# A last product with 640 channels to a partition: column groups of 32 and one store per half group

## The chip, the cores and the metric

The kernel runs on one core of one Trainium2 chip. The metric is the device time of one execution in microseconds; the median of three runs of the kernel before is 315.18 us (315.0 to 315.5). A core has five engines that run side by side and wait for each other through semaphores: PE (TensorE, matrix products; its weight loads are shown as PEld), DVE (VectorE), ACT (ScalarE), POOL (GpSimd) and SP (SyncE, which here only issues transfers). Sixteen DMA engines move data between DRAM and the on-chip memory SBUF, whose 128 rows are called partitions. PE writes its products to PSUM, a second on-chip memory of 128 partitions, and ACT or DVE read them from there.

## The reference

Two branches of the same input x (2048 tokens x 640 channels) are mixed by a gate per token:

```
x = A_x
g = sigmoid((x * gate_w).sum(-1, keepdims=True))
a = A_ref(x, wqkv, wo)        # 32 heads, each token attends to 8 tokens at a distance of 0, 2, ... 14
b = B_ref(x, ...)             # y = irfft(rfft(x, 4096) * rfft(K, 4096))[:2048] + x * Dskip, per channel
return g * a + (1 - g) * b
```

K is a filter per channel, K[d, l] = Re sum_n C[d,n] exp(dt A[d,n] l) dt B[d,n] over 192 states. The result is 2048 x 640 in bf16, 2.62 MB.

## The kernel before, in words

The kernel has two parts. The first ("main") loads x and the weights, does the attention, multiplies it by the gate, g * a, and stores that in a DRAM buffer gaS (2048 x 640, lines 487 to 506); it also stores 1 - g in omS, builds the filter K and does the first stage of the transforms. The second ("tail", the function fft_conv) finishes the long convolution and mixes. Only its end concerns the change.

The transform of 4096 points is split. A token number is t = 64 a + t2, with a from 0 to 31 and t2 from 0 to 63. In the tail, blocks fb = 0 to 7 do the second stage of the forward transforms (L1095) and the product of the two spectra on DVE (L1123, L1126). Then 20 groups of PE products (L1156) do the first inverse stage; ACT and DVE bring each from PSUM to the tile C, which lies in the buffer bufA (L511, L513). C holds, on 128 partitions, four blocks of 160 channels with 32 frequencies each: partition 32 g + f.

The last product goes from the 32 frequencies to the 32 values of a, for each t2. Its weights psi come from DRAM in four loads of 0.5 MB; a 64 x 64 weight block holds two copies of a 32 x 32 matrix on its diagonal, one for each channel block on the 64 rows, with zeros elsewhere. Before the change a product of 64 rows, 64 output columns and 160 moving columns (L1186) makes two channel blocks for one t2 at a time, in different halves of the output's 64 partitions. PE takes four of them side by side: r = 0, 1 picks the half of the rows, j = 0, 1 the half of the output columns. So an output partition is (j, channel half, a), and holds for each of its 32 tokens (t2 = 32 j + u) a row of 320 channels. The order of the channel blocks, BLOCK = (0, 2, 1, 3) at line 33, is what makes the two blocks on one partition neighbours. It is applied where x is loaded (L1026) and in the constants of the first stage (L981).

Twelve steps of two or three u each follow (TILES, L968). Each step has one PSUM tile yp of two banks out of four such tiles. "A" steps: ACT multiplies by 1 - g of the token (tile om32, one value per partition and u, L1192) into tt, and DVE adds the attention part gaF (L1195) in one go. "D" steps: DVE does both from PSUM at once (L1200). The steps write eight result tiles ot0 to ot7 of 2, 2, 6, 6, 6, 6, 2 and 2 rows, and each result tile leaves in four transfers of 32 partitions (L1213): SP issues two, POOL the other two (ACT for the last tile). A block of memory in these transfers is a row of 320 channels, 640 B.

gaF is gaS brought back into the layout of the output partitions, in eight loads of 320 KB on SP's queue (L1114), paced by the blocks fb = 3 to 6 of the forward transform. They follow the psi loads (L1111) and stand ahead of the output stores. The values 1 - g come the same way in four tiny loads on POOL's queue (L1029).

What sets the order: every step is a task of a plan (class Plan), and a string of numbers per plan (ORDER, line 54) gives the order in which tasks are recorded; the instructions of one engine run in that order. The durations and dues in the plan have no effect at run time. Waits follow from the data: an instruction waits for the writers of what it reads and the readers of what it overwrites.

Of the kernel before, what the change touches and what calls it, by code (L numbers as in the profile page):

```python
# [20 lines left out]
S = 2048  # L21
D = 640
# [7 lines left out]
SC = 512  # L30
NWARM = 22
NSC = S // SC
BLOCK = (0, 2, 1, 3)
WRDY, XRDY = (11.8, 16.0, 19.4), (8.6, 13.7, 26.7, 29.2)


# [4 lines left out]
def _attn_consts():  # L41
# [923 lines left out]


NF = 4096
TILES = ("A2", "D2", "A3 D3", "A3 A3", "D3 A3", "A3 A3", "A2", "D2")  # L968


def _fft_consts():
    w = lambda e: np.exp(-2j * np.pi * e / NF)
    t1 = np.arange(32); t2 = np.arange(64); f1 = np.arange(32); f2 = np.arange(64)
    F1 = w(64 * np.outer(t1, f1 + 0.5))
    f1c = np.zeros((32, 32, 2), np.float32)
    f1c[:, :, 0] = F1.real; f1c[:, :, 1] = F1.imag
    f1b = np.zeros((4, 32, 4, 64), np.float32)
    for g in range(4):
        f1b[g, :, g, :] = f1c.reshape(32, 64)
    f1c = f1b.reshape(128, 256)  # L980
    f1k = f1b.reshape(4, 8, 4, 256)[list(BLOCK)].transpose(1, 0, 2, 3).reshape(128, 256)  # L981
    Phi = w(t2[None, :, None] * (f1[:, None, None] + 0.5 + 64 * f2[None, None, :]))
    phis = np.zeros((64, 2, 32, 3, 2, 64), np.float32)
    for c2 in range(2):
        phis[:, c2, :, 0, c2, :] = Phi.real.transpose(1, 0, 2)
        phis[:, c2, :, 1, c2, :] = Phi.imag.transpose(1, 0, 2)
        phis[:, c2, :, 2, c2, :] = -Phi.imag.transpose(1, 0, 2)
    phis = phis.reshape(128, 32, 3, 128)
# [12 lines left out]


def fft_prefetch(ctx, tc, x, omS, keep):
    nc = tc.nc
    f1c_np, f1k_np, phi_np, gab_np, _ = _fft_consts()
    pre = ctx.enter_context(tc.tile_pool(name="ff_pre", bufs=1))
# [1 line left out]
    P["F1c"] = pre.tile([128, 256], BF16, name="F1c")  # L1008
    P["F1k"] = keep.tile([128, 256], BF16, name="F1k")
    P["GAB"] = pre.tile([128, 2, 128], BF16, name="GAB")  # L1010
    P["omF"] = pre.tile([128, 32], BF16, name="omF")
    P["xn"] = pre.tile([128, 8, D], BF16, name="xn", tag="uga")
    P["bufA"] = pre.tile([128, 20480], BF16, name="bufA")
    phi_d = nc.inline_tensor(phi_np, name="c_phi").ap()
# [7 lines left out]
    def rows(n):  # L1022
        g, h = n // 2, n % 2
        if n == 0:
            P["Usb"] = pre.tile([128, 64, 160], BF16, name="Usb", tag="uga")
        nc.gpsimd.dma_start(P["Usb"][32 * g:32 * g + 32, 32 * h:32 * h + 32], x.rearrange("(a b) d -> a b d", b=64)[:, 32 * h:32 * h + 32, 160 * BLOCK[g]:160 * BLOCK[g] + 160])  # L1026

    def gates(g):
        nc.gpsimd.dma_start(P["omF"][32 * g:32 * g + 32], omS.rearrange("(a c s) -> c a s", c=2, s=32)[g // 2])  # L1029

    def consts(_):
        nc.gpsimd.dma_start(P["F1c"][:], nc.inline_tensor(f1c_np, name="c_f1").ap())
# [13 lines left out]
def fft_conv(ctx, tc, P, big, now, pa, b, gaS, out2d):  # L1046
# [7 lines left out]
    sb = ctx.enter_context(tc.tile_pool(name="ff_sb", bufs=1))  # L1054
    Y = sb.tile([128, 2, 80, 128], BF16, name="Y")
    yv = Y[:].rearrange("p r x (g f) -> p r (x g) f", g=4)
    om32 = sb.tile([128, 32], F32, name="om32")
    psi = sb.tile([128, 64, 2, 64], BF16, name="psi")
    nc.vector.tensor_copy(om32[:], omF[:])
    gaF = P["pool"].tile([128, 32, 320], BF16, name="gaF", tag="uga")  # L1060
    gr = gaS.rearrange("(a c s) (g e) -> c g a s e", c=2, s=32, g=2)
    orr = out2d.rearrange("(a c s) (g e) -> c g a s e", c=2, s=32, g=2)
    phis, q = P["phis"], {}
    a, c = ExitStack(), ExitStack()
    wk = a.enter_context(tc.tile_pool(name="ff_wk", bufs=2, side="right"))
# [10 lines left out]
    for fb in range(8):  # L1076
# [32 lines left out]
        def paced(_, fb=fb):  # L1109
            if fb < 4:  # L1110
                nc.sync.dma_start(psi[:, 16 * fb:16 * fb + 16], psi_d[:, 16 * fb:16 * fb + 16])  # L1111
            for k in ((), (), (), (0,), (1, 2), (3, 4), (5, 6, 7), ())[fb]:
                j, h = k // 2, 16 * (k % 2)
                nc.sync.dma_start(gaF[32 * j:32 * j + 32, h:h + 16], gr[j // 2, j % 2][:, h:h + 16])  # L1114
# [30 lines left out]
    for cb in range(20):  # L1145
# [18 lines left out]
    prev, u0 = None, 0  # L1164
    tiles = [(o, c, k[0], int(k[1])) for o, c in enumerate(TILES) for k in c.split()]
    ends_, out_ = {}, {}
    for n, (o, chunk, en, w) in enumerate(tiles):
        us = range(u0, u0 + w)
        cw = sum(int(k[1]) for k in chunk.split())
        out_.setdefault(o, u0)  # L1170
        k0 = u0 - out_[o]
        u0 += w

        def fin(_, n=n, us=us, w=w, o=o, cw=cw):
            if n == 0:
                a.close(); big.close(); c.close()
                q["yps"] = ctx.enter_context(tc.tile_pool(name="ff_ps4", bufs=4, space=PSUM))
                q["wk"] = ctx.enter_context(tc.tile_pool(name="ff_wk2", bufs=6, side="right"))
            if ("ot", o) not in q:
                q["ot", o] = q["wk"].tile([128, cw, 320], BF16, name=f"ot{o}", bufs=1)  # L1180
            yp = q["yp", n] = q["yps"].tile([128, 2, 512], F32, name="yp")
            for k, u in enumerate(us):
                for ro in range(2):
                    for j in range(2):
                        for r in range(2):
                            nc.tensor.matmul(yp[64 * j:64 * j + 64, r, 160 * k:160 * k + 160], psi[64 * r:64 * r + 64, 32 * j + u, ro, :], C[64 * r:64 * r + 64, 64 * ro + 32 * j + u, :],  # L1186
                                             start=(ro == 0), stop=(ro == 1), skip_group_check=True, tile_position=(64 * r, 64 * j))

        def scale(_, n=n, us=us):
            t = q["tt", n] = q["wk"].tile([128, 3, 320], BF16, name="tt")  # L1190
            for k, u in enumerate(us):
                nc.scalar.activation(t[:, k].rearrange("p (r d) -> p r d", r=2), q["yp", n][:, :, 160 * k:160 * k + 160], ACT.Identity, scale=om32[:, u:u + 1])  # L1192

        def mix(_, n=n, us=us, w=w, o=o, k0=k0):
            nc.vector.tensor_tensor(q["ot", o][:, k0:k0 + w], q["tt", n][:, 0:w], gaF[:, us[0]:us[0] + w], ALU.add)  # L1195

        def both(_, n=n, us=us, o=o, k0=k0):
            for k, u in enumerate(us):
                r2 = lambda t: t.rearrange("p (r d) -> p r d", r=2)
                nc.vector.scalar_tensor_tensor(r2(q["ot", o][:, k0 + k]), q["yp", n][:, :, 160 * k:160 * k + 160], om32[:, u:u + 1], r2(gaF[:, u]), ALU.mult, ALU.add)  # L1200
        m = prev = pl.add(f"yp{n}", "P", 0.17 * w, fin, deps=cps, after=[prev] + (ends + paces + list(muls.values()) if n == 0 else []), acq=["yp"])
        if en == "D":
            os = pl.add(f"st{n}", "D", 0.46 * w, both, deps=[m], rel=[("yp", m)])
        else:
            v = pl.add(f"tt{n}", "A", 0.41 * w, scale, deps=[m], rel=[("yp", m)])
            os = pl.add(f"mx{n}", "D", 0.06 + 0.167 * w, mix, deps=[v])
        ends_.setdefault(o, []).append(os)
    for o, v0 in out_.items():
        q["w", o] = w = sum(int(k[1]) for k in TILES[o].split())

        def store(e, o=o, v0=v0, w=w):
            for j in ((0, 1) if e == "S" else (2, 3)):
                {"S": nc.sync, "G": nc.gpsimd, "A": nc.scalar}[e].dma_start(orr[j // 2, j % 2][:, v0:v0 + w], q["ot", o][32 * j:32 * j + 32, 0:w])  # L1213
# [219 lines left out]
```

## Time and profile before

| | |
|---|---|
| median of three runs | 315.18 us (315.0 to 315.5) |
| the profiled execution | 316.68 us, its span 314.9 us |
| PE, DVE, ACT busy | 286.3, 285.9, 285.2 us (91% each) |
| mean granted PE clock | 0.978 |
| HBM read, written | 29.60 MB, 14.01 MB |
| last product: first and last matrix product starts | 297.0 and 304.6 us |
| ACT scaling tiles (L1192), first and last start | 297.6 and 306.2 us |
| output stores issued by SP (L1213), first and last | 299.3 and 310.0 us |

The span runs from the first to the last instruction of one profiled execution. A row of the timeline gives the start, the length, the engine, the line, the operation, out<-in, and how many instructions are merged; "SPq", "POOLq" and "ACTq" are instructions of the queue itself, such as the issue of a transfer. Packets are the pieces in which DMA engines move data; a block of memory that is contiguous on both sides is one piece on the hardware queues (q1 is SP's, q10 is ACT's), while q0, POOL's, may put several together.

### The profile page before, as it was taken

Reading aid. Unit: us, or ns where it says so; the run is one execution under the profiler, and the core shown is the slowest. Engines: PE = TensorE matmul, PEld = TensorE weight load, DVE = VectorE, ACT = ScalarE, POOL = GpSimd, SP = SyncE. Lnnn points to the kernel's source line nnn. Section 1 sums busy time; section 2 is a strip of 40 time slices with the busy share of each in tenths; the row PEclk is TensorE's granted clock in tenths of the full one; section 3 lists DMA queues with packets and bytes.
Section 4 is the critical chain, followed back from the end, with each engine's and each line's share of the span. In section 5 each row is a group of like instructions: output and inputs, shape, how many; then the busy total and the mean of one; then the engine's idle time right before and its main releaser. Section 6 shows DMA issues by size and latency. Waiting matters only on the chain. (4 is left out here: it accounts for less than half of the span.)

```text
span 314.9 us, 12073 instructions
## 1 busy us (share of the span) xinstructions
PE 286.3 (91%) x5268; PEld 169.8 (54%) x5268; DVE 285.9 (91%) x381; ACT 285.2 (91%) x431; POOL 56.9 (18%) x84
## 2 busy tenths in 40 slices
PE   8799999999999999999999989789999999979740
PEld 3455543444554554555555555447668676659730
DVE  4988999999999989999999999999888899998881
ACT  2789869999999999999999999999989799997890
POOL 8722440302000001111302022020120000000072
PEclk9799999999999999999999999999999999997995
DMA  7995679286111304537795694742493366591076
GB/s 260 363 237 140 183 200 168 81 176 149 24 36 21 106 8 122 108 89 214 192 264 126 127 212 94 153 103 79 169 334 115 131 214 167 113 167 20 4 174 161
DMA packets 47182, 45.70 MB, mean 145 GB/s; under 512 B 27034, under 2 KB 40650, under 8 KB 47130
## 3 DMA queue, kind: packets, MB, share of 16 engines
q1 hardware_dynamic: 40776, 26.68, 32.7%
q0 software_dynamic: 5392, 17.53, 21.7%
q8 instruction: 41, 0.67, 0.9%
q10 hardware_dynamic: 962, 0.73, 0.8%
q14 instruction: 11, 0.09, 0.1%
HBM read 29.60 MB, written 14.01 MB: 138 GB/s over the span
## 5 line engine op out<-in xcount | busy, mean ns | idle before, releaser
L319 PE MATMUL tb<-bufA 128*128 128x512 bf16 x300 | 76.4, 390 | 1.6 <-DMA bufA<-in_A_wqkv_dram 1.2
L842 ACT ACTIVATE big<-ar 128x740 bf16<-128x740 int16 (+1 forms) x72 | 57.6, 876 | 0.2
L827 PE MATMUL ar<-Rarg,L 64*128 64x212 bf16 (+4 forms) x600 | 47.8, 251 | 5.0 <-ACT big L842 2.2
L844 ACT ACTIVATE big<-ar 128x848 bf16<-128x848 f32 x60 | 49.8, 903 | 0.5 <-PE ar L827 0.2
L319 PEld LDWEIGHTS <-bufA 128*128 128x128 bf16 x300 | 31.8, 121 | 30.3 <-issue 9.9
L453 DVE TENSOR_TENSOR pv<-vc,asb 128x2048 bf16<-128x2048 bf16 x40 | 47.7, 1217 | 0.2 <-PE tb L460 0.2
L827 PEld LDWEIGHTS <-L 64*128 64x128 bf16 x600 | 20.7, 94 | 33.7 <-issue 30.8
L864 DVE TENSOR_TENSOR pt<-big 128x1024 bf16<-128x1024 bf16 x48 | 32.2, 702 | 1.5 <-PE kps L882 0.8
L882 PEld LDWEIGHTS <-pt 128*32 128x32 bf16 (+1 forms) x2560 | 23.1, 92 | 11.6 <-issue 9.4
L882 PE MATMUL kps<-qq,pt 128*32 128x21 bf16 (+1 forms) x2560 | 28.1, 174 | 0.6 <-ACT E L511 0.3
L484 PE MATMUL tb<-wo_sb,oT 128*128 128x320 bf16 x160 | 27.7, 301 | 0.9 <-ACT ga L493 0.7
L384 DVE TENSOR_TENSOR prod<-qA,kA 128x2048 bf16<-128x2048 bf16 x20 | 23.8, 1219 | 0.4 <-PE lg L390 0.3
L511 ACT ACTIVATE sp_u<-fp 128x640 bf16<-128x640 f32 x30 | 22.4, 876 | 1.7 <-PE fp L1095 1.7
L384 DVE TENSOR_TENSOR prod<-prj 128x2048 bf16<-128x2048 bf16 x20 | 23.8, 1218 | 0.0
L460 PE MATMUL tb<-pv,ind 128*64 128x512 bf16 (+1 forms) x192 | 22.3, 350 | 0.3 <-DVE pv L453 0.3
L511 ACT ACTIVATE sp_k<-fp 128x640 bf16<-128x640 f32 x30 | 22.2, 883 | 0.4 <-PE fp L1095 0.4
L866 DVE TENSOR_TENSOR qq<-big 128x1344 bf16<-128x1344 bf16 x24 | 21.2, 884 | 0.0
L1213 POOL DMA_DIRECT2D out_dram<-ot x14 | 7.8, 560 | 71.3 <-PE yp L1186 68.8
L1095 PEld LDWEIGHTS <-PHI 128*128 128x128 bf16 x160 | 15.6, 98 | 7.8 <-issue 1.8
L377 POOL DMA_DIRECT2D vc<-vS x16 | 11.5, 726 | 44.5 <-DVE pv L453 39.6
L484 PEld LDWEIGHTS <-oT 128*128 128x128 bf16 x160 | 13.5, 97 | 8.1 <-issue 3.6
L493 ACT ACTIVATE ga<-tb,g_sb 128x320 bf16<-128x320 f32 x28 | 15.2, 570 | 0.0
(171 smaller groups left out, 525.6 us busy)
## 6 DMA issues: line engine op xcount, KB each, us to landing
vc<-vS POOLq DMA_DIRECT2D x16, 327.5 KB, 5.4
gaS<-ga SPq DMA_DIRECT2D x8, 320.0 KB
Usb<-in_A_x_dram POOLq DMA_DIRECT2D x8, 320.0 KB, 5.0
gaF<-gaS SPq DMA_DIRECT2D x8, 320.0 KB
bufA<-in_A_wqkv_dram SPq DMA_DIRECT2D x3, 800.0 KB
L<-Sprm SPq DMA_DIRECT2D x76, 30.0 KB
asb<-aS SPq DMA_DIRECT2D x16, 128.0 KB
psi<-c_psi SPq DMA_DIRECT2D x4, 512.0 KB
```

The lines of the kernel that those rows point to most:

```text
L319: nc.tensor.matmul(ppf, self.wq[:, which, kt, e::5], self.xT[:, c0 // 1024, kt, c0 % 1024:c0 % 1024 + SC], start=(kt == 0), stop=(kt == NK ...
L384: nc.vector.tensor_tensor(b[e][:], q[:, e, o:o + C].unsqueeze(1).to_broadcast([128, W, C]), win(k[:, e, :], o, W, DIL, C), ALU.mult)
L453: nc.vector.tensor_tensor(o, vw, b["asb"][:].unsqueeze(2).to_broadcast(sh), ALU.mult)
L460: nc.tensor.matmul(b["op", e][64 * a:64 * a + 64, 0:n, :], ind[:, 32:96], b["pv", e][:, w, a, 0:n, :], start=(w == 0), stop=(w == 3), skip ...
L484: nc.tensor.matmul(apf[:, :320], b["oT"][:, e, i * 128:(i + 1) * 128], wo_sb[:, e, hf * 320:(hf + 1) * 320], start=(e == 0), stop=(e == 4))
L511: nc.scalar.activation(o, i, ACT.Identity)
L827: nc.tensor.matmul(ar[:, g2, a0:a0 + ncol], L[rows, sb, gv, l0:l0 + 128], R[rows, c0:c0 + ncol], start=True, stop=True, tile_position=(64 ...
L842: nc.scalar.activation(d_[:, :, s0 * QW:s1 * QW], ar[:].bitcast(I16)[:, :, 0:2 * (s1 - s0) * QW:2], ACT.Sin, scale=SCL)
L844: nc.scalar.activation(dst[:, gp::2].rearrange("p g s n -> p g (s n)"), ar[:, :, 0:2 * EW], ACT.Exp)
L864: nc.vector.tensor_tensor(pt[:, :, k, :], gg[:, :, ::-1] if k else gg, e1, ALU.mult)
L866: nc.vector.tensor_tensor(qq[:], trg[:, :, KI:].rearrange("p a (v m) -> p a v m", v=2), exq[:, :, KI:].unsqueeze(2).to_broadcast([128, 32, ...
L882: nc.tensor.matmul(kps[32 * g:32 * g + 32, h, NM * ql:NM * ql + NM], pt[rows, k, v, :], qq[rows, k, v, :], start=(g not in started), stop= ...
```

## The change

The last product is laid out by whole rows. There are now 16 steps, one for each u from 0 to 15, with t2 = 16 j + u and j = 0 to 3. A product has 64 rows, 32 output columns and 160 moving columns; four column groups j and two row halves r stand side by side, and an outer loop g picks the channel block on the 64 rows by taking 32 of the 64 weight columns. So an output partition is (j, a) and holds 16 tokens of 640 channels; a PSUM tile yp holds one u: 320 channels in each of its two banks. There are 512 products with their weight loads in place of 256. BLOCK is gone, since the channel blocks are now in natural order.

ACT scales 640 channels in one instruction (11 in place of 22), DVE does five direct tiles of 640 in place of ten of 320, and seven adds of 640 or 1280 in place of eight of 640 or 960. The share of ACT and DVE in the tokens is the same, 11 to 5. The eight result tiles have 1, 1, 3, 3, 4, 2, 1 and 1 rows of 640. Each leaves in two transfers of 64 partitions: SP issues the one for j = 0 and 1, POOL (ACT for the last tile) the one for j = 2 and 3. In DRAM the tokens of j = 0 and j = 1 interleave: 64 a + 16 j + u. The transfer's access on the DRAM side is therefore j (2), a (32), then a contiguous run of 640 channels times the tile's rows; on the SBUF side it is 64 partitions. The gaF loads take all 128 partitions and two u at a time: on the DRAM side j (4), a (32), a contiguous run of 1280. The gate tile om16 has 16 columns.

The new lines of the product, the stores and the loads, from the diff (order strings and repeated parts cut):

```diff
-BLOCK = (0, 2, 1, 3)
...
-TILES = ("A2", "D2", "A3 D3", "A3 A3", "D3 A3", "A3 A3", "A2", "D2")
+TILES = "A", "D", "AAD", "AAD", "AADA", "AA", "A", "D"
...
-    gaF = P["pool"].tile([128, 32, 320], BF16, name="gaF", tag="uga")
-    gr = gaS.rearrange("(a c s) (g e) -> c g a s e", c=2, s=32, g=2)
-    orr = out2d.rearrange("(a c s) (g e) -> c g a s e", c=2, s=32, g=2)
+    gaF = P["pool"].tile([128, 16, D], BF16, name="gaF", tag="uga")
+    gr = gaS.rearrange("(a j s) d -> j a s d", j=4, s=16)
+    orr = out2d.rearrange("(a j s) d -> j a s d", j=4, s=16)
...
-                j, h = k // 2, 16 * (k % 2)
-                nc.sync.dma_start(gaF[32 * j:32 * j + 32, h:h + 16], gr[j // 2, j % 2][:, h:h + 16])
+                nc.sync.dma_start(gaF[:, 2 * k:2 * k + 2], gr[:, :, 2 * k:2 * k + 2])
...
+            for g in range(2):
                 for ro in range(2):
-                    for j in range(2):
+                    for j in range(4):
                         for r in range(2):
-                            nc.tensor.matmul(yp[64 * j:64 * j + 64, r, 160 * k:160 * k + 160], psi[64 * r:64 * r + 64, 32 * j + u, ro, :], C[64 * r:64 * r + 64, 64 * ro + 32 * j + u, :],
-                                             start=(ro == 0), stop=(ro == 1), skip_group_check=True, tile_position=(64 * r, 64 * j))
+                            nc.tensor.matmul(yp[32 * j:32 * j + 32, r, 160 * g:160 * g + 160], psi[64 * r:64 * r + 64, 16 * j + u, ro, 32 * g:32 * g + 32], C[64 * r:64 * r + 64, 64 * ro + 16 * j + u, :],
+                                             start=(ro == 0), stop=(ro == 1), skip_group_check=True, tile_position=(64 * r, 32 * j))
...
+                        nc.vector.scalar_tensor_tensor(r2(q["o", o]["ot"][:, k]), q["yp", u][:, :, 0:320], om16[:, u:u + 1], r2(gaF[:, u]), ALU.mult, ALU.add)
...
+                        nc.scalar.activation(r2(x["tt"][:, i]), q["yp", u][:, :, 0:320], ACT.Identity, scale=om16[:, u:u + 1])
...
+                    nc.vector.tensor_tensor(q["o", o]["ot"][:, k:k + w], x["tt"][:], gaF[:, u - w:u], ALU.add)
...
-            for j in ((0, 1) if e == "S" else (2, 3)):
-                {"S": nc.sync, "G": nc.gpsimd, "A": nc.scalar}[e].dma_start(orr[j // 2, j % 2][:, v0:v0 + w], q["ot", o][32 * j:32 * j + 32, 0:w])
+            j = 0 if e == "S" else 2
+            {"S": nc.sync, "G": nc.gpsimd, "A": nc.scalar}[e].dma_start(orr[j:j + 2, :, v0:v0 + w], q["o", o]["ot"][32 * j:32 * j + 64])
```

More of the change, by code (lines that the diff above doesn't have):

```diff
@@ L980, in _fft_consts @@
     f1c = f1b.reshape(128, 256)
-    f1k = f1b.reshape(4, 8, 4, 256)[list(BLOCK)].transpose(1, 0, 2, 3).reshape(128, 256)
+    f1k = f1b.reshape(4, 8, 4, 256).transpose(1, 0, 2, 3).reshape(128, 256)
     Phi = w(t2[None, :, None] * (f1[:, None, None] + 0.5 + 64 * f2[None, None, :]))
@@ L1010, in fft_prefetch @@
     P["GAB"] = pre.tile([128, 2, 128], BF16, name="GAB")
-    P["omF"] = pre.tile([128, 32], BF16, name="omF")
+    P["omF"] = pre.tile([128, 16], BF16, name="omF")
     P["xn"] = pre.tile([128, 8, D], BF16, name="xn", tag="uga")
@@ L1025, in rows @@
             P["Usb"] = pre.tile([128, 64, 160], BF16, name="Usb", tag="uga")
-        nc.gpsimd.dma_start(P["Usb"][32 * g:32 * g + 32, 32 * h:32 * h + 32], x.rearrange("(a b) d -> a b d", b=64)[:, 32 * h:32 * h + 32, 160 * BLOCK[g]:160 * BLOCK[g] + 160])
+        nc.gpsimd.dma_start(P["Usb"][32 * g:32 * g + 32, 32 * h:32 * h + 32], x.rearrange("(a b) d -> a b d", b=64)[:, 32 * h:32 * h + 32, 160 * g:160 * g + 160])
     def gates(g):
-        nc.gpsimd.dma_start(P["omF"][32 * g:32 * g + 32], omS.rearrange("(a c s) -> c a s", c=2, s=32)[g // 2])
+        nc.gpsimd.dma_start(P["omF"][32 * g:32 * g + 32], omS.rearrange("(a j s) -> j a s", j=4, s=16)[g])
     def consts(_):
@@ L1056, in fft_conv @@
     yv = Y[:].rearrange("p r x (g f) -> p r (x g) f", g=4)
-    om32 = sb.tile([128, 32], F32, name="om32")
+    om16 = sb.tile([128, 16], F32, name="om16")
     psi = sb.tile([128, 64, 2, 64], BF16, name="psi")
-    nc.vector.tensor_copy(om32[:], omF[:])
-    gaF = P["pool"].tile([128, 32, 320], BF16, name="gaF", tag="uga")
-    gr = gaS.rearrange("(a c s) (g e) -> c g a s e", c=2, s=32, g=2)
-    orr = out2d.rearrange("(a c s) (g e) -> c g a s e", c=2, s=32, g=2)
+    nc.vector.tensor_copy(om16[:], omF[:])
+    gaF = P["pool"].tile([128, 16, D], BF16, name="gaF", tag="uga")
+    gr = gaS.rearrange("(a j s) d -> j a s d", j=4, s=16)
+    orr = out2d.rearrange("(a j s) d -> j a s d", j=4, s=16)
     phis, q = P["phis"], {}
@@ L1163, in fft_conv @@
         cps.append(pl.add(f"cp{cb}", "AD", {"A": 0.905, "D": 1.13}, ev, deps=ms, rel=[("cy", ms[0])]))
[L1164 to L1175, printed above, removed]
+    prev, u = None, 0
@@ L1176, in fin @@
+    for o, chunk in enumerate(TILES):
+        o0, cw, done, q["o", o] = u, len(chunk), [], {}
+        def fin(_, u, o=o, cw=cw):
+            if u == 0:
                 a.close(); big.close(); c.close()
                 q["yps"] = ctx.enter_context(tc.tile_pool(name="ff_ps4", bufs=4, space=PSUM))
-                q["wk"] = ctx.enter_context(tc.tile_pool(name="ff_wk2", bufs=6, side="right"))
-            if ("ot", o) not in q:
-                q["ot", o] = q["wk"].tile([128, cw, 320], BF16, name=f"ot{o}", bufs=1)
@@ L1181, in fin @@
-            yp = q["yp", n] = q["yps"].tile([128, 2, 512], F32, name="yp")
-            for k, u in enumerate(us):
+                q["wk"] = ctx.enter_context(tc.tile_pool(name="ff_wk2", bufs=4, side="right"))
+            if "ot" not in q["o", o]:
+                q["o", o]["ot"] = q["wk"].tile([128, cw, D], BF16, name=f"ot{o}", bufs=1)
+            yp = q["yp", u] = q["yps"].tile([128, 2, 512], F32, name="yp")
+            for g in range(2):
                 for ro in range(2):
-                    for j in range(2):
+                    for j in range(4):
@@ L1185, in fin @@
                         for r in range(2):
-                            nc.tensor.matmul(yp[64 * j:64 * j + 64, r, 160 * k:160 * k + 160], psi[64 * r:64 * r + 64, 32 * j + u, ro, :], C[64 * r:64 * r + 64, 64 * ro + 32 * j + u, :],
-                                             start=(ro == 0), stop=(ro == 1), skip_group_check=True, tile_position=(64 * r, 64 * j))
[L1189 to L1211, printed above, removed]
-            for j in ((0, 1) if e == "S" else (2, 3)):
-                {"S": nc.sync, "G": nc.gpsimd, "A": nc.scalar}[e].dma_start(orr[j // 2, j % 2][:, v0:v0 + w], q["ot", o][32 * j:32 * j + 32, 0:w])
+                            nc.tensor.matmul(yp[32 * j:32 * j + 32, r, 160 * g:160 * g + 160], psi[64 * r:64 * r + 64, 16 * j + u, ro, 32 * g:32 * g + 32], C[64 * r:64 * r + 64, 64 * ro + 16 * j + u, :],
+                                             start=(ro == 0), stop=(ro == 1), skip_group_check=True, tile_position=(64 * r, 32 * j))
@@ new lines, in fft_conv, with both, scale, mix @@
+        r2 = lambda t: t.rearrange("p (r d) -> p r d", r=2)
+        k = 0
+        while k < cw:
+            en, w = chunk[k], 1
+            while en == "A" and k + w < cw and chunk[k + w] == "A":
+                w += 1
+            tts, x = [], {}
+            for i in range(w):
+                m = prev = pl.add(f"yp{u}", "P", 0.3, lambda _, f=fin, u=u: f(_, u), deps=cps, after=[prev] + (ends + paces + list(muls.values()) if u == 0 else []), acq=["yp"])
+                if en == "D":
+                    def both(_, u=u, o=o, k=k):
+                        nc.vector.scalar_tensor_tensor(r2(q["o", o]["ot"][:, k]), q["yp", u][:, :, 0:320], om16[:, u:u + 1], r2(gaF[:, u]), ALU.mult, ALU.add)
+                    done.append(pl.add(f"st{u}", "D", 0.78, both, deps=[m], rel=[("yp", m)]))
+                else:
+                    def scale(_, u=u, i=i, w=w, x=x):
+                        if i == 0:
+                            x["tt"] = q["wk"].tile([128, w, D], BF16, name="tt", tag=f"tt{w}")
+                        nc.scalar.activation(r2(x["tt"][:, i]), q["yp", u][:, :, 0:320], ACT.Identity, scale=om16[:, u:u + 1])
+                    tts.append(pl.add(f"tt{u}", "A", 0.69, scale, deps=[m], rel=[("yp", m)]))
+                u += 1
+            if en == "A":
+                def mix(_, u=u, o=o, k=k, w=w, x=x):
+                    nc.vector.tensor_tensor(q["o", o]["ot"][:, k:k + w], x["tt"][:], gaF[:, u - w:u], ALU.add)
+                done.append(pl.add(f"mx{u - w}", "D", 0.06 + 0.334 * w, mix, deps=tts))
+            k += w
@@ L1214, in fft_conv, with store @@
+        def store(e, o=o, v0=o0, w=cw):
+            j = 0 if e == "S" else 2
+            {"S": nc.sync, "G": nc.gpsimd, "A": nc.scalar}[e].dma_start(orr[j:j + 2, :, v0:v0 + w], q["o", o]["ot"][32 * j:32 * j + 64])
         for e, t_ in (("S", 0.7), ("G", 1.1) if o < len(TILES) - 1 else ("A", 0.15)):
-            pl.add(f"out{o}{e}", e, t_, store, deps=ends_[o], dma=0.165 * w)
+            pl.add(f"out{o}{e}", e, t_, store, deps=done, dma=0.33 * cw)
     pl.emit(tc)
```

4 rows, old and new, of the table ORDER are left out of this document.

## The prediction, made before the change was run

> **What bounds the kernel now.** I read first the chain of waits, then the stretches of its last 18 us, then the timeline of that stretch. The change starts where the last matrix product starts, at 297.00, so only what follows can gain or lose, apart from the loads made ready for it. Chain of waits of the kernel before (start us, us, what):
>
> ```profile
> 297.57 5.45 ACT tt L1192 x13
> 304.17 2.73 ACT tt L1192 x6
> 306.92 0.50 DVE ot L1195
> 307.70 1.64 POOL out_dram L1213 x3
> 309.35 0.56 POOLq L1428
> ```
>
> It names ACT's scaling up to 306.9, then POOL's issue. It does not follow the stores' data. The stretches (us from:to, length, busy time of PE, PEld, DVE, ACT, POOL, clock, share of the 16 DMA engines, GB/s) do:
>
> ```profile
> 299.00:300.00 1.00, 0.77 (x47) 0.61 (x40) 1.00 (x3) 1.00 (x3) 0.37 (x1) 1.00 0.00 0
> 300.00:302.00 2.00, 1.46 (x72) 1.14 (x64) 1.79 (x4) 2.00 (x6) 2.00 (x5) 1.00 0.55 136
> 302.00:304.00 2.00, 1.02 (x40) 0.76 (x40) 1.69 (x4) 2.00 (x6) 1.65 (x4) 1.00 0.91 223
> 310.00:312.00 2.00, 0.00 (x0) 0.00 (x0) 0.00 (x0) 0.00 (x0) 0.00 (x0) 0.50 0.91 243
> 312.00:313.00 1.00, 0.00 (x0) 0.00 (x0) 0.00 (x0) 0.00 (x0) 0.00 (x0) 0.50 0.15 44
> 313.00:315.00 2.00, 0.00 (x0) 0.00 (x0) 0.00 (x0) 0.00 (x0) 0.00 (x0) 0.50 0.00 0
> ```
>
> No byte of the output moves before 300.0. From 302 to 312 the DMA engines are nine tenths busy, the last data falls at about 312.5, and the span ends 2.4 us later. One busy engine carries 223/(16 x 0.91) = 15.3 GB/s there (16.7 in 310 to 312), in blocks of 640 B. So the end is set by how fast the stores drain, with ACT and DVE close ahead of them.
>
> **The change, part by part.** Compute first. Timeline of before:
>
> ```profile
> 288.29 8.49 ACT L511 ACTIVATE bufA<-cp 128x1024 bf16<-128x1024 f32 x9 [0.23 <-PE cp L1156]
> 291.11 5.74 DVE L513 CAST bufA<-cp 128x1024 bf16<-128x1024 f32 x5
> 297.00 2.59 PE L1186 MATMUL yp<-bufA,psi 64*64 64x160 bf16 x128 [1.29 <-DVE bufA L513]
> 297.57 9.32 ACT L1192 ACTIVATE tt<-yp,om 128x320 bf16<-128x320 f32 x22 [0.79 <-PE yp L1186]
> 298.80 0.48 DVE L1195 TENSOR_TENSOR ot<-tt,gaF 128x640 bf16<-128x640 bf16 x1
> 299.19 1.46 DVE L1200 SCALAR_TENSOR_TENSOR ot<-yp,om,gaF 128x320 bf16<-128x320 f32 x3
> 299.34 11.50 SPq L1213 DMA_DIRECT2D out_dram<-ot  x16
> 300.57 1.22 DVE L1195 TENSOR_TENSOR ot<-tt,gaF 128x960 bf16<-128x960 bf16 x2
> 307.33 1.00 DVE L1200 SCALAR_TENSOR_TENSOR ot<-yp,om,gaF 128x320 bf16<-128x320 f32 x2
> ```
>
> ACT: 9.32/22 = 0.424 us for 320 elements, 8.49/9 = 0.943 for 1024, so 0.424 + 320 x 0.519/704 = 0.66 us for the new 640. Eleven make 7.3 us against 9.3. DVE from PSUM: 1.46/3 = 0.487 for 320, 5.74/5 = 1.148 for 1024, so 0.79 for 640; five make 3.9 against 4.9. The adds: 0.48 for 640, 0.61 for 960, so about 0.74 for 1280; four of 1280 and three of 640 make 4.4, against six of 960 and two of 640 = 4.6. DVE is at 8.3 us instead of 9.5.
>
> PE sends 512 pairs of weight load and product instead of 256. Bounds per pair: 2.59/128 = 20 ns in the old form, and 28.1 us/2560 = 11 ns in the one other product here that has column groups of 32:
>
> ```profile
> L882 PE MATMUL kps<-qq,pt 128*32 128x21 bf16 (+1 forms) x2560 | 28.1, 174 | 0.6 <-ACT E L511 0.3 <-DVE qq L866 0.2
> ```
>
> That is 5.6 to 10.3 us for the whole product; by its 160 columns it is nearer the old form. Followed through DVE's new order (below): first tile out of ACT at 298.3, first add done at 298.8, last result at 307.2 if PE keeps up, 308.7 if each pair takes 20 ns. Before it was 308.3. Compute thus gains about 1 us, or nothing. DVE, the last result tiles, before and then now (names ot, tt, yp are result, scaled and PSUM tiles):
>
> ```order
> L1195 TENSOR_TENSOR ot_6890<-tt,gaF 128x640
> L1200 SCALAR_TENSOR_TENSOR ot_6926<-yp,om_5980,gaF 128x320 x3
> L1195 TENSOR_TENSOR ot_7131<-tt,gaF 128x960 x2
> L1195 TENSOR_TENSOR ot_7182<-tt,gaF 128x640
> L1200 SCALAR_TENSOR_TENSOR ot_7215<-yp,om_5980,gaF 128x320 x2
> ```
>
> ```order
> L1202 TENSOR_TENSOR ot_6890<-tt,gaF 128x640
> L1191 SCALAR_TENSOR_TENSOR ot_6927<-yp,om_5980,gaF 128x640
> L1202 TENSOR_TENSOR ot_7313<-tt,gaF 128x1280
> L1202 TENSOR_TENSOR ot_7384<-tt,gaF 128x640
> L1191 SCALAR_TENSOR_TENSOR ot_7421<-yp,om_5980,gaF 128x640
> ```
>
> The first add moved ahead of the direct tiles; otherwise fewer, longer rows in the same roles.
>
> Now the transfers, SP's queue before and then now (size of the side that is written, outermost count first):
>
> ```order
> L792 DMA L_190<-Sprm 40x2x192 x8
> L1114 DMA gaF<-gaS 32x16x320 x8
> L1213 DMA out_dram<-ot_6890 32x2x320 x2
> L1213 DMA out_dram<-ot_7057 32x6x320 x2
> L1213 DMA out_dram<-ot_7215 32x2x320 x2
> ```
>
> ```order
> L791 DMA L_190<-Sprm 40x2x192 x8
> L1112 DMA gaF<-gaS 128x1x1280 x8
> L1208 DMA out_dram<-ot_6890 2x32x640
> L1208 DMA out_dram<-ot_7172 2x32x2560
> L1208 DMA out_dram<-ot_7421 2x32x640
> ```
>
> Two transfers per tile and queue became one, and each block of memory at least twice as long. But the outermost count of the DRAM side went from 32 to 2 (the half group's two sets of 32 tokens lie interleaved in DRAM). What an outermost count does can be seen on the eight L transfers, whose count is 40. The DMA view of 101 to 107.7 us, when only their data moves:
>
> ```profile
> DMA  0000005200000000000300422334043241514300
> DMA packets 721, 0.26 MB, mean 39 GB/s; under 512 B 720, under 2 KB 720, under 8 KB 720
> q1 hardware_dynamic: 720, 0.25, 15.8%
> L<-Sprm SPq DMA_DIRECT2D x8, 30.0 KB
> ```
>
> Each moves 40 x 2 blocks, 640 in all. The other 80 packets are ten per transfer. The same view from 299 to 314 us, for the old stores with count 32:
>
> ```profile
> DMA  0004547798988898799699999978999799510000
> ...
> q1 hardware_dynamic: 2304, 1.31, 35.1%
> q0 software_dynamic: 576, 1.23, 31.4%
> q10 hardware_dynamic: 160, 0.08, 1.9%
> ```
>
> SP's 16 stores have 2048 blocks of 640 B and ACT's two 128, so 256/16 and 32/2: sixteen extra packets each. I read the extra packets as one completion per DMA engine used: ten for 40, sixteen for 32. Forty was cut into ten equal shares of four rows, not into sixteen uneven ones. So a transfer is cut along its outermost count into equal whole shares. By that a store whose count is 2 is two shares and runs on two engines. [...]
>
> Which two engines no row shows. Eight L transfers sent behind one another never fill a slice above 5 tenths, which ten fixed engines allow and do not prove. I take the same two for all of SP's and ACT's stores.
>
> Rate of one engine with longer blocks:
>
> ```profile
> 239.00:241.00 2.00, 1.91 (x17) 1.70 (x16) 1.78 (x3) 2.00 (x4) 0.00 (x0) 1.00 0.46 164
> 244.00:246.00 2.00, 1.31 (x11) 0.90 (x10) 1.76 (x4) 0.70 (x2) 0.00 (x0) 1.00 0.99 397
> 238.79 0.36 SPq L505 DMA_DIRECT2D gaS<-ga  x1
> 241.39 1.29 SPq L1074 DMA_DIRECT2D PHX<-c_phi  x3
> 263.75 15.85 SPq L1114 DMA_DIRECT2D gaF<-gaS  x8
> ```
>
> The gaS store in 1280 B blocks: 164/(16 x 0.46) = 22.3 GB/s per busy engine. The PHX load in 3072 B: 397/(16 x 0.99) = 25.1. The new blocks are 1280 B for the four tiles of one token, 2560 to 5120 B for the other twelve tokens: I take 23.5.
>
> Bytes on those two engines: SP's 1.31 MB and ACT's 0.08 MB are unchanged, so 1.39/2 = 0.70 MB each. POOL's 1.23 MB goes in seven stores on pairs I do not know; spread over eight pairs it adds 1.23/16 = 0.08. Bounds: none, or its largest store (4 tokens x 64 x 1280 B over two = 0.16 MB). [...]
>
> **Sum:** before, SP issued its first store at 299.34 and data moved from the fourth slice of that view (300.1 at the earliest), 0.8 us later. The first result is now ready at 298.8 instead of 299.3; I start the stores at 300.0. Two engines need 0.78 MB/23.5 GB/s = 33.2 us. They never run dry: one token takes 1.7 us, the third store is ready at 301.4. Data end 333.2, plus 2.4 = span 335.6, against the old span of 314.9. The profiled execution took 316.68, but the median of the timed runs, 315.18, lies only 0.3 above that span, so I add 0.3: **336 us**. Ends: 0.70/25.1 = 27.9 us gives 330.6; 0.86/22.3 = 38.6 gives 341.3.
>
> What costs nothing: the gaF loads have DRAM count 4 now, so four engines, 0.66 MB each at 25.1 GB/s = 26 us from 263.75, done at about 290. The first add needs the first of them at 298.3, the last add at 306.4; product and inverse transform cover them. On two engines they would end at 316, and the stores would queue behind: about 350. The gate loads (16 elements for 32 rows) are early and tiny. Compute's 1 us gain is hidden behind the stores.
>
> **Rivals.** *All sixteen engines.* If the cut goes by the 64 partitions read, or by blocks, the longer blocks win: sixteen engines carry 16 x 22.3 = 357 GB/s. When the tile of four tokens is ready at 305.1, the last eight of the sixteen tokens are still to go, 1.31 MB or 3.7 us from 305.9: data end 309.6, span 312.0, time 312.3, or up to 314 if PE paces at 20 ns a pair. For it: the L transfers count 40 on both sides, so they do not show what happens where one side counts 2 and the other 64. Against: their ten shares follow the outermost count, not the 80 blocks. [...] *Two engines, but another pair for each transfer.* Then the largest store decides: ready at 305.1, moving at 305.9, 0.164 MB/23.5 = 7.0, data end 312.9, span 315.3, time 315.6: no change. Its turning point is the pairs overlapping: as soon as SP's stores share one pair, the forecast holds. For it: only that no row names engines; against it: the slices of the L transfers, which changing sets of ten could have filled further.
>
> **How the numbers follow.** Same two engines 0.86, all sixteen 0.08, changing pairs 0.06. The forecast's own range is 330.6 to 341.3; I widen it by 4 us on both sides, since the start, the rate alone on two engines and POOL's share are estimates: 326 to 345, which leaves out the two rivals and a little more. A difference under 0.2% (0.6 us) cannot be told from none in runs that spread from 315.0 to 315.5. Faster 0.08, same 0.05, slower 0.87.
>
> **What would show it.** In the changed kernel: DMA share near 0.12 (two engines of sixteen) at about 45 to 50 GB/s from 316 on, once POOL's stores are through, while every compute engine is done by 307 to 309; two extra packets per store instead of sixteen; four per gaF load, and these loads still moving past 285. The time is wrong if the share stays near 0.9 after 302 and the data end before 311 (all sixteen), or if the share falls but the data end at 313 (changing pairs).

## The result, and the profile after

The changed kernel takes 343.24 us (median of 6 runs, 340.27 to 345.82) against 315.09 us for the kernel before on the same chip (314.02 to 318.55): a ratio of 1.0857, 95% interval 1.0773 to 1.0942. It is slower by about 28 us; the prediction said 336 us with a range of 326 to 345. The ratio is that of the means, without the changed kernel's one slow run (345.82 us). Its profiled execution took 340.41 us with a span of 338.6. In the later timed runs, too, a time stands 1.8 us above its own span (315.6 and 317.41, 312.4 and 314.15), so 1.8 is what lies around the span.

The stretches of the changed kernel's last part (us from:to, length, busy time of PE, PEld, DVE, ACT, POOL, clock, share of the 16 DMA engines, GB/s):

```profile
298.00:300.00 2.00, 1.58 (x128) 1.35 (x128) 1.21 (x3) 1.72 (x3) 1.14 (x2) 1.00 0.21 48
300.00:302.00 2.00, 0.04 (x2) 0.00 (x0) 2.00 (x3) 1.11 (x2) 0.31 (x1) 1.00 0.52 112
302.00:304.00 2.00, 1.02 (x71) 1.03 (x79) 0.42 (x2) 0.00 (x0) 0.35 (x1) 0.77 0.40 85
308.00:310.00 2.00, 0.00 (x0) 0.00 (x0) 1.29 (x2) 0.29 (x1) 0.88 (x2) 0.50 0.46 126
312.00:314.00 2.00, 0.00 (x0) 0.00 (x0) 0.00 (x0) 0.00 (x0) 0.00 (x0) 0.50 0.31 87
320.00:325.00 5.00, 0.00 (x0) 0.00 (x0) 0.00 (x0) 0.00 (x0) 0.00 (x0) 0.50 0.14 52
325.00:330.00 5.00, 0.00 (x0) 0.00 (x0) 0.00 (x0) 0.00 (x0) 0.00 (x0) 0.50 0.13 50
333.00:335.00 2.00, 0.00 (x0) 0.00 (x0) 0.00 (x0) 0.00 (x0) 0.00 (x0) 0.50 0.11 42
337.00:339.00 2.00, 0.00 (x0) 0.00 (x0) 0.00 (x0) 0.00 (x0) 0.00 (x0) 0.50 0.00 1
```

Where the old kernel had a share of about 0.9 from 302 to 312, this one has 0.3 to 0.6 and, from 320 on, about 0.13 at 50 GB/s: two engines of sixteen, 25 GB/s each. In the last 2 us of the data, from 335 on, it is 0.07 at 25 GB/s, which is one engine. No compute engine works in all that time. The DMA view of the stores, 297 to 338 us (first the busy tenths in 40 slices, then the queues):

```profile
DMA  0134535334255543322121111111111111110000
...
q0 software_dynamic: 1776, 1.24, 14.0%
q1 hardware_dynamic: 528, 1.31, 9.0%
q10 hardware_dynamic: 66, 0.08, 0.5%
```

SP's eight stores have 512 blocks, so 16 packets more, two for each; ACT's one has 64 and two more. Before it was sixteen for each.

The chain of waits, again, does not follow the stores' data. It ends at 309.77 on POOL's queue, 29 us before the span does:

```profile
307.56 0.66 POOL out_dram L1208
308.22 0.87 issue
309.09 0.68 POOLq L1423
```

The second half of the story is hidden behind the stores. The timeline of the last product and what it feeds:

```profile
294.59 1.90 PE L1178 MATMUL yp<-bufA,psi 64*32 64x160 bf16 x160 [1.28 <-DVE bufA L512]
296.00 0.49 DVE L1202 TENSOR_TENSOR ot<-tt,gaF 128x640 bf16<-128x640 bf16 x1 [1.56 <-ACT tt L1197]
296.56 31.23 SPq L1208 DMA_DIRECT2D out_dram<-ot  x8
297.34 0.52 PE L1178 MATMUL yp<-bufA,psi 64*32 64x160 bf16 x34 [0.85 <-DVE ot L1191]
298.42 1.61 PE L1178 MATMUL yp<-bufA,psi 64*32 64x160 bf16 x128 [0.56 <-issue]
302.98 2.30 PE L1178 MATMUL yp<-bufA,psi 64*32 64x160 bf16 x128 [2.94 <-issue]
304.24 2.17 ACT L1197 ACTIVATE tt<-yp,om 128x640 bf16<-128x640 f32 x3 [3.13 <-PE yp L1178]
306.70 1.26 PE L1178 MATMUL yp<-bufA,psi 64*32 64x160 bf16 x62 [1.43 <-issue]
308.73 0.88 DVE L1191 SCALAR_TENSOR_TENSOR ot<-yp,om,gaF 128x640 bf16<-128x640 f32 x1
```

From 298.42 on PE works in blocks of exactly 128 pairs (256 instructions; the last block is the 62 that remain) and stands still between them for nothing that this view shows; ACT waits for PE, and DVE for ACT. The last result comes 15.0 us after the product's start (309.61 - 294.59), against 11.3 before (308.33 - 297.00).

### The profile page after: what moved, and what is told of

The parts are those of the page before. It is cut to its first block, busy times and chain, and to the rows that moved or that the text cites. A ratio compares the mean times of both kernels' runs of the same rounds, so it can differ in the third digit from the quotient of the medians.

```text
span 338.6 us, 12554 instructions
## 1 busy us (share of the span) xinstructions
PE 286.2 (85%) x5524; PEld 169.8 (50%) x5524; DVE 285.1 (84%) x375; ACT 283.5 (84%) x420; POOL 53.8 (16%) x77
## 4 chain that ended last, share of the span: by engine, by line
PE 35%; issue 26%; ACT 20%; POOL 5%; DVE 3%; DMA 2%; POOLq 0%; SPq 0%; ACTq 0%; DVEq 0%
PE tb L318 9%; PE ar L826 7%; ACT big L843 7%; ACT big L841 6%; PE kps L881 5%; PE tb L459 4%; PE tb L483 4%; PE lg L389 2%; POOL L L767 2%; PE bp L1324 2%; POOL out_dram L1208 1%; ACT L841 1%; DMA Sprm<-pc 1%; PE bp L1320 1%; POOL L L765 1%
## 5 line engine op out<-in xcount | busy, mean ns | idle before, releaser
L318 PE MATMUL tb<-bufA 128*128 128x512 bf16 x300 | 75.0, 384 | 1.5 <-DVE kA L342 0.4
L318 PEld LDWEIGHTS <-bufA 128*128 128x128 bf16 x300 | 31.7, 120 | 29.0 <-issue 8.8
L483 PEld LDWEIGHTS <-oT 128*128 128x128 bf16 x160 | 13.5, 97 | 8.1 <-issue 3.6
L1208 POOL DMA_DIRECT2D out_dram<-ot x7 | 4.7, 673 | 75.5 <-PE yp L1178 67.5
L841 ACT ACTIVATE bufA<-ar 128x740 bf16<-128x740 int16 (+1 forms) x18 | 15.2, 879 | 0.0
```

The lines of the kernel that those rows point to most:

```text
L318: nc.tensor.matmul(ppf, self.wq[:, which, kt, e::5], self.xT[:, c0 // 1024, kt, c0 % 1024:c0 % 1024 + SC], start=(kt == 0), stop=(kt == NK ...
L483: nc.tensor.matmul(apf[:, :320], b["oT"][:, e, i * 128:(i + 1) * 128], wo_sb[:, e, hf * 320:(hf + 1) * 320], start=(e == 0), stop=(e == 4))
L841: nc.scalar.activation(d_[:, :, s0 * QW:s1 * QW], ar[:].bitcast(I16)[:, :, 0:2 * (s1 - s0) * QW:2], ACT.Sin, scale=SCL)
```

## The experiments

The start of the last product moves between 294.6 and 297.4 from one execution to the next, so two things are compared inside each trace: the stores' data time (first to last store packet in the trace's packet records) and the time from the product's start to the last result. A run given without a number of runs was executed once; the six times of the changed kernel span 5.5 us, so a difference of one or two microseconds between two such runs says little. In the diffs, `...` marks what is left out.

**Both stores cut in two.** Nothing but the stores changes; the DRAM count is 32 again, the long blocks stay.

```diff
-            j = 0 if e == "S" else 2
-            {...}[e].dma_start(orr[j:j + 2, :, v0:v0 + w], q["o", o]["ot"][32 * j:32 * j + 64])
+            for j in ((0, 1) if e == "S" else (2, 3)):
+                {...}[e].dma_start(orr[j, :, v0:v0 + w], q["o", o]["ot"][32 * j:32 * j + 32])
```

> Only the stores differ from the changed kernel: each half-group store of 2 x 32 x (640 w) goes as two of 32 x (640 w), so the outermost DRAM count is 32 again and the blocks stay 1280 to 5120 B; all compute is the changed kernel's. Theory (a transfer is cut into equal shares along its outermost count, so count 2 meant two engines): sixteen completions per store, DMA share above 0.7 for some microseconds instead of 0.13, and the whole drain behind 313 is gone. In the changed kernel's profiled times the last result came 14.8 us after the product's start at 294.8; with 2 us of transfer, 1.5 us of tail and 1.8 us around the span that is 315 us if PE's waits for issue stay (8.2 us in the product), 312 us if they shrink with the stores. Rival A (the long blocks, or the interleaved order in DRAM, are slow in themselves): still 330 us or more, since neither changes. Rival B (PE's waits for instructions delay the stores and set the end): no better than 335.

Measured: 317.37 us (6 runs), a ratio to the kernel before of 1.0078 (1.0047 to 1.0109). Its DMA view, 295 to 314 us, and one stretch:

```profile
DMA  0000100126658899495889107869989600357610
...
q1 hardware_dynamic: 768, 1.31, 25.6%
```

```profile
308.00:310.00 2.00, 1.26 (x62) 0.94 (x62) 0.19 (x1) 0.79 (x1) 0.88 (x2) 0.50 1.02 346
```

256 packets more than blocks for SP's sixteen stores, sixteen each again, and 346 GB/s in one stretch. So 26 of the 28 us hang on two lines of code, and on the cut alone: compute, block lengths and the place of the tokens in DRAM are the changed kernel's. Both rivals fall. What is left, 0.8%, is taken up below; the theory's 315 was 2 us short, 1.1 of which is the later start of the product in this execution (295.87; the expectation had 294.8).

**Only SP's stores cut; only POOL's and ACT's cut.**

```diff
+            if e != "S":
+                {...}[e].dma_start(orr[2:4, :, v0:v0 + w], q["o", o]["ot"][64:128])
+                return
+            for j in (0, 1):
+                nc.sync.dma_start(orr[j, :, v0:v0 + w], q["o", o]["ot"][32 * j:32 * j + 32])
```

> Of the changed kernel only SP's stores are cut into two of 32 rows of tokens; POOL's seven and ACT's one keep the count 2. Theory (SP's stores shared two fixed engines; POOL's go to pairs that change): the drain is that of POOL's largest store, 0.164 MB on each of two engines at 23.5 GB/s = 7.0 us behind its issue at about 307, plus 1.5 and 1.8: 317 to 320 us. Rival (POOL's stores share one pair as SP's do): 1.23 MB on two engines, 0.61 MB / 23.5 = 26 us from 299: 328 to 331 us.

> Of the changed kernel only POOL's and ACT's stores are cut into two of 32; SP's eight keep the count 2. Theory (all of SP's stores on the same two engines): 1.31 MB / 2 = 0.66 MB at 23.5 GB/s = 27.9 us from 297.8, plus POOL's even share of 1.23/16 = 0.08 MB = 3.3 us, plus 1.5 and 1.8: 332 us, and two engines alone busy (share 0.12) behind 313. Rival (the pair changes from store to store; the slow end of the changed kernel came from POOL's): 315 to 318 us.

With POOL's and ACT's cut and SP's not: 333.37 us, 31.5 us of data (31.2 by the terms in the expectation). That is SP's stores sharing two engines for the whole 1.31 MB (a share of 0.12 to 0.13 at 51 to 54 GB/s from 314 to 325). With SP's cut alone: 325.49 us, between the two expectations. Two stretches of that run, and the queues' rows of its DMA view from 312 to 314:

```profile
312.00:314.00 2.00, 0.00 (x0) 0.00 (x0) 0.00 (x0) 0.00 (x0) 0.00 (x0) 0.50 0.53 128
320.00:322.00 2.00, 0.00 (x0) 0.00 (x0) 0.00 (x0) 0.00 (x0) 0.00 (x0) 0.50 0.06 18
```

```profile
q0 software_dynamic: 130, 0.17, 38.0%
q1 hardware_dynamic: 40, 0.09, 15.1%
```

Its largest POOL store in the DMA view (how many, KB, us from issue to landing):

```profile
out_dram<-ot POOLq DMA_DIRECT2D x1, 320.0 KB, 13.5
```

POOL's packets (q0) alone take 38% of the engines there and move 0.17 MB in 2 us, where two engines at 25 GB/s would move 0.10; so POOL's stores do not share one pair. But the store of four tokens took 13.5 us from its issue (306.66) to landing and not 7. My expectation had it alone on its pair; by the later runs, which show it for the changed kernel, its pair is also that of ACT's store, and SP's stores now have sixteen extra packets each (768 packets for 512 blocks). What each pair carried in this run was not taken apart.

**One transfer of all 128 partitions for each tile, all by SP.** The DRAM count is four.

```diff
+            if e == "S":
+                nc.sync.dma_start(orr[:, :, v0:v0 + w], q["o", o]["ot"][:])
```

> One transfer of all 128 partitions for each tile, all on SP's queue, none on POOL's and ACT's: the outermost DRAM count is 4, with the same blocks of 1280 to 5120 B. Theory (engines = outermost count): four engines, DMA share about 0.25 behind 302, four completions per store; 2.62 MB / 4 = 0.66 MB at 23.5 GB/s = 27.9 us from 297.8, plus 1.5 and 1.8: 329 us. Rival (a queue, not the count, limits: SP alone carries what SP carried at 1.31 MB in 39 us): about 78 us of drain, 378 us. Rival (the count does not matter): share above 0.7 and 312 to 316 us.

Measured: 330.47 us, 29.4 us of data. The DMA view of 296 to 332 us:

```profile
DMA  0022322232232222222222222222222211000000
...
q1 hardware_dynamic: 1056, 2.62, 20.1%
```

1024 blocks and 32 extra packets, four for each of eight stores, with a steady quarter of the engines (0.25 to 0.26 from 308 to 325). All 2.62 MB go through one queue faster than the changed kernel's go through three (29.4 us against 39.36). In these runs the time follows the count, not the queue, and not the number of bytes in a transfer; nor does it follow the partitions on the SBUF side, of which 128 gave four engines here (share 0.25), 64 two (0.13) and 32 up to all sixteen (1.02).

**POOL's part of the two engines.** Three runs leave stores of POOL out (the left-out part of the output is not written): all seven; the last three; the last two.

```diff
+            if e == "G":                 # all; `and o > 3`: the last three; `and o > 4`: the last two
+                return
```

> Of the changed kernel the seven stores of POOL are left out (1.23 MB of the output is not written); SP's eight and ACT's one are unchanged. Theory (SP's and ACT's stores share two engines, and nothing else runs there): 1.31 + 0.08 = 1.39 MB, 0.70 MB each, at 23.5 GB/s = 29.6 us of data from 297.8 on, 331 us; at the 26 GB/s of undisturbed long packets 26.8 us, 328 us. The difference to the changed kernel's 39.35 us of data is then what POOL's stores cost on these two engines. Rival (POOL's stores do not touch these engines): 39 us, as with them, 340 us.

> Of the changed kernel POOL's last three stores are left out (the tiles of four, two and one tokens; 0.57 MB of the output is not written); its first four (one, one, three and three tokens), SP's and ACT's are unchanged. Theory (POOL's stores go to pairs of engines in turn, and the tile of four tokens is the one that lands on SP's and ACT's pair): data take the 29.6 us that they took without POOL, up to 31, and the time is 331 to 333 us. Rival (what POOL adds is spread over all its stores, by their bytes): 0.66 of 1.23 MB, so 5.2 of the 9.75 us, 34.8 us of data and 336 to 337 us.

> Of the changed kernel POOL's last two stores are left out (two tokens and one, 0.25 MB not written); its store of the tile of four tokens is made, unlike in the run beside it. Theory (that store is on SP's and ACT's pair): 0.164 MB at 23.5 GB/s = 7.0 us more than without it, 36.5 to 38 us of data, 338 to 339 us. Rival (by bytes): 0.98 of 1.23 MB, 7.8 of 9.75 us, so 37.4 us here but 34.8 us without it; rival (the excess comes from the stores behind it): 30 to 31 us of data, 332 us.

| POOL's stores, tokens | stores' data, us | step, us |
|---|---|---|
| none | 29.65 (298.48 to 328.13) | |
| 1, 1, 3, 3 | 31.70 (299.46 to 331.16) | 2.05 |
| 1, 1, 3, 3, 4 | 38.21 (298.25 to 336.47) | 6.5 |
| all seven (the changed kernel) | 39.36 (297.79 to 337.15) | 1.15 |

The times are 331.39, 334.42 and 339.73 us. One stretch of the run without POOL, and from the DMA view of the run with five of its stores the landing of the largest:

```profile
312.00:314.00 2.00, 0.00 (x0) 0.00 (x0) 0.00 (x0) 0.00 (x0) 0.00 (x0) 0.50 0.13 54
```

```profile
out_dram<-ot POOLq DMA_DIRECT2D x1, 320.0 KB, 19.2
```

Without POOL the share is about 0.13 from 304 to 327 (0.12 to 0.15) and the data take 29.65 us, which is 0.70 MB at 23.5 GB/s. That the average agrees to the digit is in part luck: the two engines together moved 51 to 58 GB/s from 306 to 320 and 45 from 320 to 327, and for the last microsecond one of them was through (24 GB/s).

The store of four tokens alone adds 6.5 us of the 9.7; its 0.164 MB per engine would take 7.0. So it lies on SP's pair, and by-bytes (34.8 and 37.4, where 31.7 and 38.2 came) falls. The changed kernel's own trace agrees. Its queues' rows from 320 to 326, and SP's from 326 to 330:

```profile
q1 hardware_dynamic: 32, 0.16, 6.2%
q0 software_dynamic: 44, 0.11, 5.4%
q10 hardware_dynamic: 31, 0.04, 1.7%
```

```profile
q1 hardware_dynamic: 53, 0.19, 12.1%
```

Up to 326, when the store of four tokens lands (305.86 + 20.0), the three queues share 13.3% of the engines, which is two; behind it SP's queue has nearly all of the two.

So one store of POOL met SP's pair (6.5 us), and the four ahead of it mostly did not. Those four cost 2 us (2.05) in these single runs and not nothing; which engines they ran on is not shown.

**The gaF loads with a count of 32.** On top of both stores cut.

```diff
-                nc.sync.dma_start(gaF[:, 2 * k:2 * k + 2], gr[:, :, 2 * k:2 * k + 2])
+                j, h = k % 4, 8 * (k // 4)
+                nc.sync.dma_start(gaF[32 * j:32 * j + 32, h:h + 8], gr[j, :, h:h + 8])
```

> Both stores and gaF loads have an outermost DRAM count of 32: on top of the kernel whose stores were cut in two, each of the eight gaF loads takes 32 partitions and eight tokens instead of 128 partitions and two. Theory (the loads on four engines cost nothing, since they land by 292 to 293 and the first add needs them at 296 to 297): the same time as with the stores alone cut, 317.4, within 1 us. Rival (the loads' long stay on four engines delays psi or other work of the stage): 1 us or more faster, 316 or less.

Measured: 318.96 us, a ratio of 1.0127 (1.0091 to 1.0164) where the stores alone gave 1.0078 (1.0047 to 1.0109). The loads now run at a share of 0.56 to 0.73 and are through by 285, and nothing is won; the median is 1.6 us worse, outside the expectation of 1 us, but on another chip and with intervals of the ratios that overlap. So the four engines of the gaF loads (0.26 to 0.29 in the changed kernel) cost nothing, as predicted. Whether the quick loads cost something was not followed up.

**What is left: PE's supply of instructions.** Two runs on top of both stores cut. In one every store waits for the last result. In the other PE makes the product with 256 pairs of 320 columns instead of 512 of 160 (the values of half the channels are other ones by that; all else is the same work).

```diff
-            for g in range(2):
+            for g in range(1):
...
-        matmul(yp[32 * j:32 * j + 32, r, 160 * g:160 * g + 160], psi[...], C[64 * r:64 * r + 64, 64 * ro + 16 * j + u, :], ...)
+        i = min(64 * ro + 16 * j + u, 126)
+        matmul(yp[32 * j:32 * j + 32, r, 0:320], psi[...], C[64 * r:64 * r + 64, i:i + 2, :].rearrange("p a d -> p (a d)"), ...)
```

> On top of the kernel whose stores were cut in two, every store waits for the last result: SP and POOL issue the last tile's stores first and the other tiles' behind it, so no output moves while the product runs. Theory (the 16 KB of instructions come at their own pace, whatever else the DMA engines do): PE's waits for issue in the product stay at 6 to 9 us and the last result still comes 13 to 15 us behind the product's start. Rival (stores on the same DMA engines hold the instructions up): the waits fall to 4 us or less, as in the kernel before the change, and the last result comes about 11 us behind the start. The time itself is 2.62 MB at about 350 GB/s = 7.5 us behind the last result, 320 to 323 us.

> On top of the kernel whose stores were cut in two, the last product is made with half of the instructions: for each token row and column group one pair of weight load and product over 320 columns of two neighbouring rows instead of two pairs over 160, so 256 pairs instead of 512, and as many columns in all. The values of the output are wrong by that (the second half of the channels is made with the wrong rows); everything behind PSUM is the same work. Theory (PE runs dry of instructions: the instruction queue brings 16 KB, which is 128 pairs, every 3.5 to 5 us, and the product needs four of them): two of them, PE's waits for issue fall from 8.7 to 3 to 5 us, the last result comes 3 to 4 us earlier, 313 to 314.5 us. Rival (ACT, DVE or the stores set the pace): within 0.7 us of 317.4.

The waits of PE's weight loads in the product, first with every store late, then with half the instructions (line, what for, us in total, times, longest; "issue" is a wait for nothing that the profile shows), and the instruction queue's row of the DMA view of each, 296 to 312 and 295 to 310 us:

```profile
PEld L1178 <- issue: 8.1, 6, 2.3
q8 instruction: 4, 0.07, 1.4%
```

```profile
PEld L1179 <- issue: 5.5, 7, 1.4
q8 instruction: 2, 0.03, 0.8%
```

With no store under way the DMA engines carry nothing but four packets of 16 KB, and PE still waits 8.1 us; the last result comes 15.1 us after the start. So the stores do not hold the instructions up. The packets of 16 KB tell where each stop ends: in all ten traces with 512 pairs, each of the last three blocks starts 1.2 to 1.6 us after such a packet has landed. In the changed kernel packets land at 297.03, 301.76 and 305.34, and the blocks start at 298.42, 302.98 and 306.70.

With half the instructions the last result comes 10.5 us after the start, and the time is 314.02 us (10 runs), a ratio of 0.9984 (0.9947 to 1.0022). The expectation was 313 to 314.5 us with waits of 3 to 5 us; the waits were a little longer (5.5), the effect was as said. The late stores gave 327.88 us where 320 to 323 were expected: their 2.62 MB took 10.8 us (313.0 to 323.8), at 242 GB/s and not 350; POOL's issues alone took 7.4 us of that.

| | product start to last result, us | weight loads' waits for issue, us | time, us |
|---|---|---|---|
| before (256 pairs) | 11.3 | 3.9 | 315.09 |
| the change (512 pairs) | 15.0 | 8.2 | 343.24 |
| four engines (512) | 14.1 | 7.1 | 330.47 |
| stores cut (512) | 15.2 | 8.7 | 317.37 |
| stores cut and late (512) | 15.1 | 8.1 | 327.88 |
| stores cut, 256 pairs of 320 columns | 10.5 | 5.5 | 314.02 |

(The times come from several chips; the kernel before gave 314.3 to 315.1 us beside them.)

The supply of instructions sets most of it; neither the stores nor ACT nor DVE do. A part may be PE's clock: in the changed kernel the block at 302.98 took 2.30 us at a granted clock of 0.50 and the one at 298.42 took 1.61 at 1.00. By that ratio the last two blocks would be 1.1 us shorter in all at a clock of 1.00; this is an estimate, and no run separates it from the supply. No version here beats the kernel before: with 512 pairs the layout by whole rows loses on PE what its longer blocks could win.

## Why the prediction was right, point by point

- **Two engines by the outer count, the same two for SP and ACT:** shown. Two extra packets per store, share 0.13 at 50 GB/s, and by the two runs around it: count 32 brings 26 of 28 us back, count 4 gives four engines (0.25). That SP and ACT share the pair shows in the run without POOL: ACT's store is issued at 309.18, and from 308 to the end of the data the share stays at 0.14 or less, where a third and fourth engine would have brought it to 0.25. The sign of 0.12 "from 316 on" came only from 320 on (0.21 and 0.18 before it), since POOL's data moved until 326.
- **0.70 MB at 23.5 GB/s:** 29.65 us without POOL, as worked out, as an average over faster and slower stretches.
- **POOL's share, 0.08 MB or 3.4 us:** this is the term that was mis-sized. It measured 9.7 us, 6.5 of them one store. The upper of the two bounds, the largest store on this pair (0.16 MB, 7.0 us), fits what that store measured, and I took the even share instead, an estimate that no run shows. Even that bound leaves 2 us for the earlier four stores and 1 for the last two, which single runs do not settle.
- **The sum:** start 300.0 was 297.79 (-2.21, the execution's earlier product), the drain 33.2 was 39.36 (+6.16), the tail 2.4 was 1.48 (-0.92), and around the span 0.3 was 1.78 (+1.48): 335.9 + 4.5 = 340.4, the profiled 340.41. So the drain was off by more than the total, and an earlier start, which nothing in the sum foresaw, took a part of it back: that much is luck. The 0.3 came from setting a median of other runs against one profiled span; before's own 316.68 - 314.9 = 1.8 was in front of me. The median of the timed runs lies 2.8 us higher still, without a trace of that. It is outside the forecast's own range, which ended at 341.3, and inside the stated one only by the 4 us of widening.
- **Compute done by 307 to 309, gaining about 1 us:** wrong, hidden by the stores. The last result came at 309.61 with the product starting 2.4 us earlier than in the profile before, so 3.7 us were lost. The step that failed is PE's 5.6 to 10.3 us for 512 pairs: it took 13.4 (294.59 to 307.96). Both bounds were the pace of pairs that follow each other without a stop; neither knew a supply of instructions, for which PE stood still 4.9 us. The other terms were about a tenth too low: ACT 2.16/3 = 0.72 us for 0.66, DVE from PSUM 0.88 for 0.79, the add of 1280 0.82 for 0.74.
- **gaF for nothing:** right; four engines (0.26 to 0.29 from 270 to 292) and past 285:

```profile
285.00:290.00 5.00, 4.34 (x134) 3.89 (x135) 5.00 (x8) 5.00 (x7) 0.00 (x0) 1.00 0.28 106
292.00:294.00 2.00, 1.30 (x44) 1.06 (x37) 2.00 (x3) 2.00 (x3) 0.00 (x0) 1.00 0.08 31
```

  They are through shortly after 292, not at 290, with the first add at 296.00.
- **The rival of all sixteen engines, 312.3 to 314:** the run with the stores cut is that rival made true, and it gave 317.4. Had sixteen engines come, the sum would have failed at the same PE term. With that term out of the way (256 wide pairs) it gave 314.0.
- **Changing pairs, 315.6:** refuted for SP by the run with only POOL's and ACT's cut (share 0.12 to 0.13 from 314 on, 333.37 us); for POOL the pairs do change (38% of the engines at once, where one pair would be 12.5%).

## What to carry to other kernels

Before longer blocks are counted as a gain, look at the outermost count of the transfer's DRAM side: here 2 in place of 32 cost 26 of the 28 us, and for the stores that SP and ACT issue the extra packets per transfer in the DMA view went with the engines that were busy (2 with a share of 0.13, 4 with 0.25, 16 with up to 1.02). Cut along the next count, with twice the issues, the same stores gave 317.37 us in place of 343.24. And when a layout doubles PE's instructions in a short stage, price the instructions themselves (here a block of 128 pairs every 3.4 to 4.8 us), not only the array.

## What the runs showed of the hardware that was not expected

- **Instructions come to PE 256 at a time.** In the run with the stores cut, blocks of 128, 128 and 62 pairs start at 299.64, 303.64 and 308.19, 4.0 and 4.6 us apart, where the first two are 1.61 and 2.00 us long. Over its whole span the changed kernel has 43 packets of 16 KB on the instruction queue and 11048 weight loads and products on PE, 257 to a packet; the kernel before has 41 and 10536, again 257. What sets the pace, and how far ahead PE asks for a packet, is not shown.
- **PE's clock in a product that is fed this way.** The same 128 pairs took 1.61 us at a granted clock of 1.00 and 2.30 at 0.50. It fell in 302 to 304 here (0.77), and with half the instructions only in 304 to 306 (0.87). That the gaps cause it was not tested.
- **POOL's stores with count 2 leave more than their data.** 1776 packets in place of 576 for the same 1.23 MB, 1568 of them of 16 bytes or less (the number in the row of q0 in the DMA view of the result, the sizes in the trace's packet records). The same stores cut to count 32 left 480. Their own time is small, some 14 us summed over all engines; what they are is open.
